# Chunk 0's output projection as seven block products woven into chunk 1, and the keys' copies of batch 2 on ScalarE

## The chip, the cores and the metric

The kernel runs on one core of one Trainium2 chip. The metric is the device time of one execution in microseconds (us). Executions of the same kernel mostly agree within 0.3%, so differences of half a microsecond need several rounds and, better, the trace. An execution that takes over 1.5% more than the fastest of the same kernel counts as slow and is left out of the comparisons; the others are called fast.

## The reference

The program is an attention whose keys and values are first averaged over groups of eight positions, followed by a gated feed-forward layer.

```python
batch, heads, seq, dim = 8, 8, 576, 64
k_p, v_p = mean over 8 positions of k, v            # 72 keys and values per head
attn = softmax(q @ k_p^T / sqrt(dim))               # with max subtraction
x = (attn @ v_p), heads side by side                # 4608 tokens x 512
out = (max(x @ w_gate, 0) * (x @ w_val)) @ w_out    # d_ff = 1536, float32 out
```

## The kernel before

The 4608 tokens are worked through in nine chunks of 512. Chunk c's gate and value products stand between the attention of batch c+1 (scores, values, transposes) and the output projection of chunk c-1.

A gate unit is eight products of 512 columns, a relu on ScalarE and a multiplication on VectorE. It takes two of four PSUM banks (`ps_mm`):

```python
def gate_val(c, fo, t0=0, n=TCH):
    ...
    for w in (wg_sb, wv_sb):
        t = ps_mm.tile([P, TCH], F32, name="mm_ps", tag="mm_ps")
        ... # matmuls of w with x_T into t
    nc.scalar.activation(out=relu[:, :n], in_=ps[0][:, :n], func=AF.Relu)
    nc.vector.tensor_tensor(out=h_tiles[c][:, fo, t0:t0 + n], in0=ps[1][:, :n], in1=relu[:, :n], op=ALU.mult)
```

From chunk 1 on the output projection is a 2x2 block product done with seven block products instead of eight (the scheme of Strassen and Winograd). It needs four differences of the weights (`weight_sums`, twelve VectorE operations, once) and four sums of blocks of h per chunk (eight VectorE operations with two operands in SBUF). One PSUM bank (`ps_acc`) holds the running product:

```python
def add(k, x, y, op, half):
    nc.vector.tensor_tensor(out=S[k][:, i], in0=x[:, i], in1=y[:, i], op=op)
...
def pr1():
    nc.scalar.copy(p1, product(a, e, True))
def pr2():
    nc.scalar.copy(rows[0][:, :, :HD], product(b, g, False))
def pr6():
    plus(u2, product(S[1], T[1], True), p1)
# pr7, pr4, pr5, pr3 follow in the same way, with VectorE additions
```

Chunk 0 alone used plain rows, twelve 512-column products per block of 128 tokens, in two halves (`o`), copied out by VectorE. At the handover from chunk 0 to chunk 1 the halves alternate with batch 1's last five pieces of values `V` and their transposes `x`:

```python
run([... pv[0], z[10], *Sc[14:], pv[1], z[11], V[4], o[0], V[0], x[4], o[1], V[1], x[0]])
q_dma(2)
run([o[2], V[2], x[1], o[3], x[2], V[3], o[4]])
prep_k(2, True)      # GpSimd: sums batch 2's keys, issues batch 3's loads
prep_v(2)            # GpSimd: sums batch 2's values
```

`z[i]` and `a[i]` are half gate units of chunk 0, `pv` the pooled values. A piece passes VectorE (reciprocal, multiplication), TensorE (transpose) and ScalarE (copy into `x_T`), and chunk 1's first gate unit needs x[4], x[0], x[1] and x[2].

The softmax here doesn't subtract the row's maximum and nothing guards it: scores larger than these inputs give would overflow.

Of the kernel before, what the change touches and what calls it, by code (L numbers as in the profile page):

```python
# [9 lines left out]
F32 = mybir.dt.float32  # L10
# [6 lines left out]
def kernel(  # L17
# [10 lines left out]
    nc = tc.nc  # L28
# [4 lines left out]
    DM = H * D  # L33
    DFF = moe_w_gate.shape[1]
    NTOK = B * S
    P = 128
# [200 lines left out]
    def run(pieces):  # L237
        for piece in pieces:
            piece()
# [26 lines left out]
    def k_transposes(b):  # L266
        ps = ps_mm.tile([P, KJ + 1, KROWS], F16, name="mm_ps", tag="mm_ps")
        k_windows(b, ps, 0, KJ + 1)
        eng = nc.scalar if b > 2 else nc.vector
        k_evacuate(b, ps, False, eng)  # L270
        k_evacuate(b, ps, True, eng)

# [183 lines left out]
        n, j = divmod(t, 2)  # L456
        eng.dma_start(out=out_cols_of[LAST, j, :, n * IQ:(n + 1) * IQ, cols], in_=o)

    def out_rows(c, ts, eng=None):

        cell = []

        def part(lo, hi):
            if not cell:
                cell.append(ps_mm.tile([P, DM], F32, name="mm_ps", tag="mm_ps"))
            t = cell[0]
            for fo in range(lo, hi):
                nc.tensor.matmul(  # L468
                    out=t, lhsT=h_tiles[c][:, fo, ts * P:(ts + 1) * P], rhs=wo_sb[:, fo, :],
                    start=(fo == 0), stop=(fo == n_fo - 1),  # L470
                )
            if hi == n_fo:
                o = fout_pool.tile([P, DM], F32, name="fout")
                if eng is nc.vector:
                    eng.tensor_copy(out=o, in_=t)
                else:
                    nc.scalar.copy(o, t)
                store(o, c * TCH + ts * P)

        return [lambda: part(0, n_fo // 2), lambda: part(n_fo // 2, n_fo)]  # L480



    sends = []
# [14 lines left out]
    def out_products(c, last=False):  # L499


        hc = h_tiles[c]
        a, d1 = hc[:, :n_hf, :HT], hc[:, :n_hf, HT:]
        b, d = hc[:, n_hf:, :HT], hc[:, n_hf:, HT:]
        S = [sum_pool.tile([P, n_hf, HT], F16, name=f"sum{i}") for i in range(4)]
        e, g, h = wo_sb[:, :n_hf, :HD], wo_sb[:, n_hf:, :HD], wo_sb[:, n_hf:, HD:]
        T = [wo_sums[:, i] for i in range(4)]
        p1, u2, u3 = [mid_pool.tile([P, 2, HD], F32, name=f"mid{i}") for i in range(3)]
        rows = [half_pool.tile([P, 2, DM], F32, name=f"rows{i}", bufs=2 - i) for i in range(2)]
        cell = {}  # L510

        def add(k, x, y, op, half):
            i = slice(half * n_hf // 2, (half + 1) * n_hf // 2)
            nc.vector.tensor_tensor(out=S[k][:, i], in0=x[:, i], in1=y[:, i], op=op)  # L514

        def product(lhs, rhs, first):
            if first:
                cell["ps"] = ps_acc.tile([P, 2, HD], F32, name="acc_ps", tag="acc_ps")
            ps = cell["ps"]
            for tb in range(2):  # L520
                for i in range(n_hf):

                    nc.tensor.matmul(  # L523
                        out=ps[:, tb, :], lhsT=lhs[:, i, tb * P:(tb + 1) * P], rhs=rhs[:, i, :],
                        start=(first and tb == 0 and i == 0), stop=(tb == 1 and i == n_hf - 1),
                        skip_group_check=True,
                    )
            return ps

        def plus(out_ap, x, y):  # L530
            nc.vector.tensor_tensor(out=out_ap, in0=x, in1=y, op=ALU.add)  # L531

        def send(half):

            def stores():
                for tb in range(2):
                    store(rows[half][:, tb, :], c * TCH + half * HT + tb * P)

            if c + 2 < n_chunks:
                sends.append(stores)  # L540
            else:
                stores()

        def pr1():
            nc.scalar.copy(p1, product(a, e, True))

        def pr2():
            nc.scalar.copy(rows[0][:, :, :HD], product(b, g, False))

        def pr6():  # L550
            plus(u2, product(S[1], T[1], True), p1)

        def pr7():
            plus(u3, product(S[2], T[2], False), p1)

        def pr4():
            if last:
                plus(rows[1][:, :, :HD], product(d, T[3], True), u3)
                send(1)
            else:  # L560
                plus(rows[1][:, :, :HD], product(d, T[3], False), p1)

        def pr5():
            plus(rows[1][:, :, HD:], product(S[0], T[0], True), u3)
            if not last:
                send(1)

        def pr3():
            plus(rows[0][:, :, HD:], product(S[3], h, False), u2)
            send(0)  # L570

        sums = [lambda k=k, x=x, y=y, op=op, half=half: add(k, x, y, op, half)
                for k, x, y, op in ((0, d1, d, ALU.add), (1, S[0], a, ALU.subtract),
                                    (2, a, d1, ALU.subtract), (3, b, S[1], ALU.subtract))
                for half in range(2)]
        order = [pr1, pr2, pr6, pr7, pr5, pr3, pr4] if last else \
            [pr1, pr2, pr6, pr7, pr4, pr5, pr3]
        return order, sums

    def last_products(c):  # L580
# [292 lines left out]
        trios = [Sc[i:i + 3] for i in range(0, 2 * H, 3)]  # L873
        return [[kt]] + [[]] * (b + 1 < B) + trios + [[p] for p in V], []

    def weave_units(units, others):

        n, m, seq = len(others), len(units), []
        for i, unit in enumerate(units):
            seq += [unit] + others[i * n // m:(i + 1) * n // m]  # L880
        return seq

    with tc.manual_schedule():
        nc.scalar.preload_act_table_set("natural_log_exp_and_others")
        nc.vector.memset(warm_sb, 0.0)
# [52 lines left out]
        half = TCH // 2  # L938
        a = [lambda fo=fo: gate_val(0, fo, 0, half) for fo in range(n_fo)]
        z = [lambda fo=fo: gate_val(0, fo, half, half) for fo in range(n_fo)]  # L940
        o = [p for ts in range(TCH // P) for p in out_rows(0, ts, nc.vector)]
        pv = [lambda half=half: pool_v_array(1, half) for half in range(2)]


# [36 lines left out]
        def kt():  # L981
# [7 lines left out]
        V = [lambda t=t: values(1, t) for t in range(n_pc)]  # L989
        x = [lambda t=t: back(1, t, nc.scalar) for t in range(n_pc)]  # L990

        run([z[3], z[4], z[5], a[6], qt[0], a[7], qt[1], qt[2], kt, z[6], z[7], a[8], *Sc[:4],
             z[8], *Sc[4:6], a[9], *Sc[6:8], z[9], *Sc[8:10], a[10], *Sc[10:12], a[11], *Sc[12:14],
             pv[0], z[10], *Sc[14:], pv[1], z[11], V[4], o[0], V[0], x[4], o[1], V[1], x[0]])
        q_dma(2)
        run([o[2], V[2], x[1], o[3], x[2], V[3], o[4]])
        prep_k(2, True)
        prep_v(2)

# [3 lines left out]
        for c in range(1, n_chunks):  # L1003
            gv = [lambda fo=fo: gate_val(c, fo) for fo in range(n_fo)]

            if c == 1:
                sums = weight_sums()
                units = weave_units(gv[:-1], o[5:])
            elif c < C_HIDDEN:
                prods, sums = out_products(c - 1)  # L1010
                units = []
                order = range(n_fo - 1)
                if c == C_HIDDEN - 1:

                    order = [fo for fo in range(n_fo) if fo % n_hf > 1]
                for fo in order:
                    if c == C_HIDDEN - 1 and len(prods) == 2:
                        units.append(gv[fo])
                        continue
                    units.append(gv[fo])  # L1020
                    if prods and fo not in (1, 4, 7, 10):
                        units.append(prods.pop(0))
            else:
                last = c == n_chunks - 1
                prods, sums = out_products(c - 1, last)
                units = []
                for fo in range(0, n_hf - 2 * last, 2):

                    if sums:
                        mine = [sums.pop(0) for _ in range(4)]  # L1030
                    else:
                        mine = x_sums_of(c + 1)
                    n = 2 if fo else 3
                    units += hidden_round(c, fo, prods[:n], mine)
                    del prods[:n]
                if last:

                    tail, last_sums = [], []

                    def begin_tail():  # L1040
                        products, ready = last_products(c)
                        tail.append(products)
                        last_sums.extend(ready)
                        run(ready[0])

                    units += [gv[n_hf - 2], prods.pop(0), begin_tail,
                              gv[n_fo - 2], lambda: run(last_sums[1]), prods.pop(0),
                              gv[n_hf - 1]]
                else:

                    gv[-1] = lambda: None
# [12 lines left out]
            for i, unit in enumerate(units):  # L1064
# [3 lines left out]
                    prep_v(c + 2)  # L1068
                unit()
                if c == 1:  # L1070
                    run(sums[i:i + 1])
                elif i in SUMS_AT and sums:
                    sums[SUMS_AT.index(i)]()
                if i in (0, 1) and sends:
# [45 lines left out]
```

## Time and profile before

| | before |
|---|---|
| median of 3 runs | 329.39 us (329.09 to 329.70) |
| profiled span | 327.4 us |
| first piece V[4] at TensorE | 49.32 us |
| chunk 1's first gate unit | 58.17 us |
| chunk 2's first gate unit | 87.34 us |

The three marks are starts of TensorE instructions in the timeline. They cut the span in four stages: what lies ahead, the handover (8.85 us), chunk 1 (29.17 us) and the rest (240.05 us).

One place shows why the keys' copies were to move. The timeline of VectorE before, then of TensorE (start, length, engine, line, operation, and in brackets the idle time with its releaser, that is, what ended it):

```profile
62.73 1.03 DVE L494 TENSOR_TENSOR wo_sums<-wo_sb 128x512 f16<-128x512 f16 x1
63.68 0.74 DVE L264 COPY kpT0l<-mm_ps 64x576 f16<-64x576 f16 x1
64.44 0.76 DVE L264 COPY kpT0u<-mm_ps 64x576 f16<-64x576 f16 x1
```

```profile
63.88 1.03 PE L430 MATMUL mm_ps<-x_T,wg_sb 128*128 128x512 f16 x4
65.26 1.04 PE L430 MATMUL mm_ps<-x_T,wv_sb 128*128 128x512 f16 x4 [0.35 <-DVE kpT0u L264]
```

The copies stand behind a weight sum. The bank that they empty is the one that the value half of the fourth gate unit needs, so TensorE stands still for 0.35 us. A bracket understates a delay, because rows of TensorE overlap in this view. A row of four 512-column products is listed with 1.03 us, but without a wait the next row starts 0.86 us after its start.

### The profile page before, as it was taken

The page shows a single profiled execution, that of the slowest core. Times are in us where ns is not written, and L with a number is a line of the kernel's source. Part 1 is how long each engine was busy: PE and PEld are TensorE (multiplying, and loading weights), DVE is VectorE, ACT ScalarE, POOL GpSimd, SP SyncE. Part 2 cuts the span into 40 slices and gives each one's busy share as a digit, 9 for nine tenths or more (in the row PEclk, how much of TensorE's full clock was granted, in tenths as well). Part 3 has the DMA queues.
Part 4 walks back from the last instruction along what each step waited for, and adds up shares of the span by engine and source line. Part 5 has one row for each costly group of instructions (what it writes and reads, how often), then busy time and mean ns, then how long its engine had stood idle before and what let it go on. Part 6 is the DMA issues. An engine that isn't in the chain of part 4 may idle for free.

```text
span 327.4 us, 7013 instructions
## 1 busy us (share of the span) xinstructions
PE 318.7 (97%) x2670; PEld 226.9 (69%) x2670; DVE 226.2 (69%) x482; ACT 151.2 (46%) x353; POOL 206.9 (63%) x258
## 2 busy tenths in 40 slices
PE   8899999999999999999999999999999999999995
PEld 3577885455566656665898867655667888888674
DVE  7465737677684864696387745784779989879762
ACT  1454482364466226612672257225825565565330
POOL 8556607999999942965199309999901577667300
PEclk9999999999999999999999999999999999999999
DMA  7999998996958538999794472223012130130035
GB/s 110 186 203 202 200 211 151 200 173 118 187 101 159 100 91 86 78 154 160 159 169 76 87 104 60 33 47 124 3 24 50 34 96 2 22 111 2 10 112 137
DMA packets 51010, 35.46 MB, mean 108 GB/s; under 512 B 30432, under 2 KB 45024, under 8 KB 50976
## 3 DMA queue, kind: packets, MB, share of 16 engines
q0 software_dynamic: 18304, 18.88, 36.5%
q1 hardware_dynamic: 32528, 16.00, 26.2%
q8 instruction: 21, 0.34, 0.4%
q10 hardware_dynamic: 144, 0.13, 0.1%
q14 instruction: 13, 0.11, 0.1%
HBM read 37.75 MB, written 9.44 MB: 144 GB/s over the span
## 4 chain that ended last, share of the span: by engine, by line
PE 89%; DVE 6%; DMA 2%; issue 1%; POOL 1%; ACT 0%; DVEq 0%; POOLq 0%
PE mm_ps L430 42%; PE acc_ps L523 19%; PE mm_ps L742 9%; PE at_ps L311 4%; PE mm_ps L468 3%; PE at_ps L389 3%; PE mm_ps L602 2%; DMA q<-in_q_dram 2%; PE at_ps L742 2%; DVE px L395 1%; DVE sum L514 1%; DVE h L439 1%; PE mm_ps L412 1%; PE mm_ps L366 1%; DVE px L758 1%
## 5 line engine op out<-in xcount | busy, mean ns | idle before, releaser
L439 DVE TENSOR_TENSOR h<-mm_ps,relu 128x512 f16<-128x512 f32 (+1 forms) x96 | 59.8, 624 | 69.5 <-PE mm_ps L430 59.2
L436 ACT ACTIVATE relu<-mm_ps 128x512 f16<-128x512 f32 (+1 forms) x96 | 52.2, 544 | 100.1 <-PE mm_ps L430 94.6
L430 PE MATMUL mm_ps<-x_T,wv_sb 128*128 128x512 f16 (+1 forms) x432 | 88.4, 332 | 0.4 <-DVE kpT0u L264 0.4
L430 PE MATMUL mm_ps<-x_T,wg_sb 128*128 128x512 f16 (+1 forms) x432 | 88.5, 331 | 0.0
L430 PEld LDWEIGHTS <-wv_sb 128*128 128x128 f16 x432 | 42.1, 98 | 31.2 <-DVE kpT0u L264 0.8
L430 PEld LDWEIGHTS <-wg_sb 128*128 128x128 f16 x432 | 38.9, 97 | 19.7 <-issue 0.3
L325 ACT ACTIVATE expT<-at_ps 72x288 f16<-72x288 f32 (+2 forms) x128 | 38.8, 374 | 14.3 <-PE at_ps L311 14.2
L523 PEld LDWEIGHTS <-sum 128*128 128x128 f16 x336 | 32.0, 98 | 6.3 <-DVE sum L514 0.9
L395 DVE TENSOR_TENSOR px<-at_ps,prd 128x256 f16<-128x256 f32 (+1 forms) x80 | 33.8, 423 | 2.7
L181 POOL TENSOR_TENSOR tree_b<-tree_a 72x256 f32<-72x256 f32 (+1 forms) x42 | 33.5, 797 | 3.3
L764 POOL TENSOR_TENSOR h<-px 128x256 f16<-128x256 f16 x36 | 25.4, 718 | 13.8 <-ACT px L761 12.8
L175 POOL TENSOR_TENSOR tree_a<-k_in 96x512 f32<-96x512 f16 x18 | 21.5, 1196 | 15.2 <-DMA k_in<-in_k_dram 15.2
L523 PE MATMUL acc_ps<-wo_sums,sum 128*128 128x256 f16 x252 | 30.9, 272 | 0.0
L175 POOL TENSOR_TENSOR tree_a<-v_in 72x512 f32<-72x512 f16 x24 | 28.7, 1197 | 0.1
L523 PEld LDWEIGHTS <-h 128*128 128x128 f16 x252 | 23.7, 98 | 2.9
L763 POOL TENSOR_SCALAR px<-px 128x256 f16<-128x256 f16 x12 | 13.0, 1080 | 18.1 <-PE mm_ps L742 15.3
L844 POOL COPY gate<-h 128x1 f16<-128x1 f16 x4 | 1.5, 380 | 33.9 <-DVE h L439 33.9
L523 PE MATMUL acc_ps<-wo_sb,h 128*128 128x256 f16 x168 | 20.6, 272 | 0.0
L514 DVE TENSOR_TENSOR sum<-h 128x768 f16<-128x768 f16 x28 | 19.0, 679 | 0.0
L531 DVE TENSOR_TENSOR rows<-acc_ps,mid 128x512 f32<-128x512 f32 x21 | 14.4, 686 | 4.7 <-PE acc_ps L523 4.6
L389 PEld LDWEIGHTS <-expT 72*128 72x128 f16 (+1 forms) x280 | 12.9, 100 | 5.9 <-DVE prd L394 0.8
L394 DVE RECIPROCAL prd<-at_ps 128x4 f32<-128x4 f32 (+1 forms) x80 | 13.7, 171 | 3.7 <-PE at_ps L389 3.6
(144 smaller groups left out, 527.9 us busy)
## 6 DMA issues: line engine op xcount, KB each, us to landing
out_dram<-rows SPq DMA_DIRECT2D x24, 256.0 KB
k_in<-in_k_dram POOLq DMA_DIRECT2D x7, 576.0 KB, 7.0
q<-in_q_dram POOLq DMA_DIRECT2D x7, 576.0 KB, 10.0
v_in<-in_v_dram POOLq DMA_DIRECT2D x6, 576.0 KB, 12.7
wg_sb<-in_moe_w_gate_dram POOLq DMA_DIRECT2D x6, 256.0 KB, 11.0
wv_sb<-in_moe_w_val_dram POOLq DMA_DIRECT2D x6, 256.0 KB, 10.8
wo_sb<-in_moe_w_out_dram POOLq DMA_DIRECT2D x3, 512.0 KB, 10.7
v_in<-in_v_dram POOLq DMA_DIRECT2D x2, 512.0 KB, 11.9
```

The source lines that it names most:

```text
L175: eng.tensor_tensor(out=cell["a"][:n], in0=src[:, :, :4 * D], in1=src[:, :, 4 * D:], op=ALU.add)
L181: eng.tensor_tensor(out=cell["c"][:n], in0=a[:n, :, :2 * D], in1=a[:n, :, 2 * D:], op=ALU.add)
L325: nc.scalar.activation(out=out_ap, in_=in_ap, func=AF.Exp, scale=EXP_SCALE)
L389: nc.tensor.matmul(out=ps[:n, c0:c0 + D + 1], lhsT=weights(b, h, t), rhs=stats[b % 2][:SP, g, s0:s0 + D + 1], start=True, stop=True,)
L395: nc.vector.tensor_tensor(out=x[:n, half * NG // 2:(half + 1) * NG // 2, :, :], in0=pv.rearrange("p g (x c) -> p g x c", x=2)[:, :, :, :D] ...
L430: nc.tensor.matmul(out=t[:, lo:hi], lhsT=w[:, ci, fsl], rhs=x_T[:, ci, x0:x0 + hi - lo], start=(ci == 0), stop=(ci == n_co - 1),)
L436: nc.scalar.activation(out=relu[:, :n], in_=ps[0][:, :n], func=AF.Relu)
L439: nc.vector.tensor_tensor(out=h_tiles[c][:, fo, t0:t0 + n], in0=ps[1][:, :n], in1=relu[:, :n], op=ALU.mult)
L514: nc.vector.tensor_tensor(out=S[k][:, i], in0=x[:, i], in1=y[:, i], op=op)
L523: nc.tensor.matmul(out=ps[:, tb, :], lhsT=lhs[:, i, tb * P:(tb + 1) * P], rhs=rhs[:, i, :], start=(first and tb == 0 and i == 0), stop=(tb ...
L742: nc.tensor.matmul(out=ps[key][:, m], lhsT=w_of(m)[:, i], rhs=xs[:, i], start=(first and m == 0 and i == 0), stop=(m == 1 and i == N_CO - ...
L764: nc.gpsimd.tensor_tensor(out=hc[:, fo_out, cols], in0=gv[:, 0], in1=gv[:, 1], op=ALU.mult)
```

## The change

The intent is to save an eighth of chunk 0's projection work on TensorE and to free VectorE of the keys' copies. The first two products are cut into four parts of six matmuls, which take the old halves' place in the handover; the other five go whole between chunk 1's gate units. Half of the weight sums moves ahead, into chunk 0. The sums of h go behind chunk 1's first units.

```diff
 def k_transposes(b):
-        eng = nc.scalar if b > 2 else nc.vector
+        eng = nc.scalar
 ...
+        if c == 0:
+            order[:2] = [lambda pr=pr, tb=tb: pr((tb,)) for pr in order[:2] for tb in range(2)]
 ...
-             pv[0], z[10], *Sc[14:], pv[1], z[11], V[4], o[0], V[0], x[4], o[1], V[1], x[0]])
+             pv[0], *w_sum[:3], z[10], *Sc[14:], pv[1], *w_sum[3:6], z[11], V[4]])
+        prods, sums = out_products(0)
+        run([prods[0], V[0], x[4], prods[1], V[1], x[0]])
         q_dma(2)
-        run([o[2], V[2], x[1], o[3], x[2], V[3], o[4]])
+        run([prods[2], V[2], x[1], prods[3], x[2], V[3]])
 ...
-                units = weave_units(gv[:-1], o[5:])
+                units = gv[:4] + prods[4:5] + gv[4:6] + prods[5:6] + gv[6:8] + prods[6:7] + \
+                    gv[8:9] + prods[7:8] + gv[9:11] + prods[8:]
+                at = [sums[:2], sums[2:3], sums[3:4], w_sum[6:7], [w_sum[7], sums[4]],
+                      [w_sum[8], sums[5]], w_sum[9:10], w_sum[10:11], w_sum[11:], [], [], [],
+                      sums[6:7], sums[7:]]
 ...  # out_rows and weave_units removed; pr1 and pr2 take a list of blocks
-                    run(sums[i:i + 1])
+                    run(at[i] if i < len(at) else [])
```

`at[i]` is what VectorE gets behind unit i: `sums[:2]`, two sums of h, come behind chunk 1's very first gate unit.

More of the change, by code (lines that the diff above doesn't have):

```diff
@@ L457, in store_cols @@
         eng.dma_start(out=out_cols_of[LAST, j, :, n * IQ:(n + 1) * IQ, cols], in_=o)
-    def out_rows(c, ts, eng=None):
-        cell = []
-        def part(lo, hi):
-            if not cell:
-                cell.append(ps_mm.tile([P, DM], F32, name="mm_ps", tag="mm_ps"))
-            t = cell[0]
-            for fo in range(lo, hi):
-                nc.tensor.matmul(
-                    out=t, lhsT=h_tiles[c][:, fo, ts * P:(ts + 1) * P], rhs=wo_sb[:, fo, :],
-                    start=(fo == 0), stop=(fo == n_fo - 1),
-                )
-            if hi == n_fo:
-                o = fout_pool.tile([P, DM], F32, name="fout")
-                if eng is nc.vector:
-                    eng.tensor_copy(out=o, in_=t)
-                else:
-                    nc.scalar.copy(o, t)
-                store(o, c * TCH + ts * P)
-        return [lambda: part(0, n_fo // 2), lambda: part(n_fo // 2, n_fo)]
     sends = []
@@ L514, in add, with product @@
             nc.vector.tensor_tensor(out=S[k][:, i], in0=x[:, i], in1=y[:, i], op=op)
-        def product(lhs, rhs, first):
-            if first:
+        def product(lhs, rhs, first, blocks=(0, 1)):
+            if first and 0 in blocks:
                 cell["ps"] = ps_acc.tile([P, 2, HD], F32, name="acc_ps", tag="acc_ps")
             ps = cell["ps"]
-            for tb in range(2):
+            for tb in blocks:
                 for i in range(n_hf):
@@ L542, in send, with pr1, pr2 @@
                 stores()
-        def pr1():
-            nc.scalar.copy(p1, product(a, e, True))
-        def pr2():
-            nc.scalar.copy(rows[0][:, :, :HD], product(b, g, False))
+        def pr1(blocks=(0, 1)):
+            ps = product(a, e, True, blocks)
+            if 1 in blocks:
+                nc.scalar.copy(p1, ps)
+        def pr2(blocks=(0, 1)):
+            ps = product(b, g, False, blocks)
+            if 1 in blocks:
+                nc.scalar.copy(rows[0][:, :, :HD], ps)
         def pr6():
@@ L874, in attention @@
         return [[kt]] + [[]] * (b + 1 < B) + trios + [[p] for p in V], []
-    def weave_units(units, others):
-        n, m, seq = len(others), len(units), []
-        for i, unit in enumerate(units):
-            seq += [unit] + others[i * n // m:(i + 1) * n // m]
-        return seq
     with tc.manual_schedule():
@@ L940 @@
         z = [lambda fo=fo: gate_val(0, fo, half, half) for fo in range(n_fo)]
-        o = [p for ts in range(TCH // P) for p in out_rows(0, ts, nc.vector)]
         pv = [lambda half=half: pool_v_array(1, half) for half in range(2)]
@@ L990 @@
         x = [lambda t=t: back(1, t, nc.scalar) for t in range(n_pc)]
+        w_sum = weight_sums()
         run([z[3], z[4], z[5], a[6], qt[0], a[7], qt[1], qt[2], kt, z[6], z[7], a[8], *Sc[:4],
              z[8], *Sc[4:6], a[9], *Sc[6:8], z[9], *Sc[8:10], a[10], *Sc[10:12], a[11], *Sc[12:14],
-             pv[0], z[10], *Sc[14:], pv[1], z[11], V[4], o[0], V[0], x[4], o[1], V[1], x[0]])
+             pv[0], *w_sum[:3], z[10], *Sc[14:], pv[1], *w_sum[3:6], z[11], V[4]])
+        prods, sums = out_products(0)
+        run([prods[0], V[0], x[4], prods[1], V[1], x[0]])
         q_dma(2)
-        run([o[2], V[2], x[1], o[3], x[2], V[3], o[4]])
+        run([prods[2], V[2], x[1], prods[3], x[2], V[3]])
         prep_k(2, True)
@@ L1006 @@
             if c == 1:
-                sums = weight_sums()
-                units = weave_units(gv[:-1], o[5:])
+                units = gv[:4] + prods[4:5] + gv[4:6] + prods[5:6] + gv[6:8] + prods[6:7] + \
[3 more added lines that the diff above has]
+                      sums[6:7], sums[7:]]
             elif c < C_HIDDEN:
```

## The prediction

> **What bounds the kernel now.** I read the page first. Its busy line and its clock row say that TensorE sets the time and that no throttle disturbs it:
>
> ```profile
> PE 318.7 (97%) x2670; PEld 226.9 (69%) x2670; DVE 226.2 (69%) x482; ACT 151.2 (46%) x353; POOL 206.9 (63%) x258
> ...
> PE   8899999999999999999999999999999999999995
> ...
> PEclk9999999999999999999999999999999999999999
> ```
>
> The reader is to see that in all of the 40 slices but the first and the last TensorE is at least nine tenths busy. So a change pays only if it takes TensorE work away, or one of the few TensorE gaps, and does not open new ones. Next I asked for the waits between 40 and 120 us, where chunk 0's output projection lies:
>
> ```profile
> PE mm_ps L430 <- DVE kpT0u L264: 0.4, 1, 0.4
> ...
> PE at_ps L311 <- ACT expT L325: 0.2, 1, 0.2
> ```
>
> These are the only two TensorE waits there: one gap of 0.35 us at 65.26 us (a gate product waits for a PSUM bank that the copy of batch 2's keys holds), and 0.2 us that the change does not touch. Then I read the chain of work in order of time, where each piece is one run of TensorE instructions (start, length, line, count):
>
> ```profile
> 53.51 1.29 PE mm_ps L468 x6
> 54.80 0.25 PE at_ps L389 x8
> 55.05 0.23 PE mm_ps L412 x4
> 55.27 1.29 PE mm_ps L468 x6
> 56.57 0.22 PE mm_ps L412 x4
> 56.79 0.25 PE at_ps L389 x8
> 57.04 1.30 PE mm_ps L468 x6
> 58.34 1.73 PE mm_ps L430 x8
> ```
>
> L468 is half of a row block of the old output projection: six 512-column products in 1.30 us, 216 ns each. L389 computes one piece of attention values, L412 transposes a piece, L430 is the first gate and value unit of chunk 1. Before 58 us the old halves serve as filler: each 1.30 us covers the time in which VectorE normalises a piece and ScalarE copies its transpose.
>
> **What the Trainium skill says.** "TensorE: Matmul & The Clock Gate", section "Back-to-back issue gap", gives N/2.4 + 2.5 ns for a warm matmul of N columns: 216 ns for 512 and 109 for 256. The trace agrees with both: 1.30/6 = 216 ns here, and the seven-product form of later chunks takes 1.31 us for its twelve 256-column products, 109 ns each. The saving is therefore the plain arithmetic one. The same page's table at the top says that VectorE and ScalarE work strictly in order; this trace fits it (at 62.73 us a weight sum stands ahead of the keys' copies, which start at 63.68), and it is why I place every added operation in a queue. "SBUF — State Buffer", section "Who interferes with whom", says that a VectorE instruction with two SBUF inputs contends with GpSimd's reads. The trace fits: the weight sums take 0.416 us at best and 1.106 at worst while GpSimd works.
>
> **The change part by part.**
>
> *TensorE work.* Removed: 8 halves x 1.30 = 10.40 us. Added: 7 products x 1.31 = 9.17 us. Net -1.23 us.
>
> *The keys' copies of batch 2.* They leave VectorE, where they ran from 63.68 to 65.20 (0.74 + 0.76 us) behind a 1.03 us weight sum. On ScalarE such a copy takes 0.63 us (the row of batch 3 at 89.57), and at that moment ScalarE only has a 0.60 us relu every 1.73 us. Two copies end some 1.3 us after the transposes, so the 0.35 us gap should go: -0.35 us.
>
> *VectorE.* In the stretch 58 to 87 us it is busy 20.7 us of 29. Leaving: two copies of keys (1.5), three of four row copies in some part (about 1.4 of them in this stretch, at 0.69), and half of the weight sums (six at a mean of 0.67 = 4.0), which move to 46 to 49 us. Coming: eight sums of h at 0.68 (5.4) and five additions from PSUM at 0.69 (3.4). 20.7 - 6.9 + 8.8 = 22.6 us, 72% of a stretch of some 31.5 us; chunk 2, which already runs this form, has 23.0 of 32 and no gap above 0.3 us. So VectorE should keep up.
>
> *The early weight sums.* At 46.1 and 48.0 us VectorE has idle times of 1.48 and 1.49 us; GpSimd is idle there too, so three sums at 0.42 = 1.26 us fit in each. The second three need the last third of the output weights. Its landing is given as 8.9 to 12.5 us after issues at 33.6 to 35.1, that is 47.6 at the latest: just in time, without margin.
>
> *The handover from chunk 0 to chunk 1, 49.3 to 58.2 us.* Here the choice lies. Before, five halves (6.5 us) stand between five pieces of values and four transposes. After, only four half products of six 256-column matmuls, 0.655 us each, 2.6 us. TensorE's own work is then 4.9 us, but the pieces now wait for each other. I followed the queues with the trace's durations: reciprocal and multiply of one piece take VectorE 1.11 us at the least; a piece is ready 1.52 us after its first product (0.33 until VectorE starts, 1.19 until the second multiply ends); a transposed piece is in place 1.0 us after its transposes start (0.42 + 0.58); a ScalarE copy out of PSUM takes 0.60 and starts 0.2 after its products.
> - First piece 49.32, half product 49.70 to 50.36, second piece to 50.63, its transpose waits for VectorE until 51.05: +0.4.
> - The fourth six products, which add onto the same bank, wait for ScalarE's copy of the first product (52.13 to 52.73): the third half product starts at 52.78, +0.37.
> - The transposes of the piece that chunk 1 needs last start at 55.0, +0.45; ScalarE copies the second product (54.77 to 55.37) ahead of them, so they are in place at 56.0, and the first gate unit waits from 55.47: +0.58.
>
> It starts at 56.05 instead of 58.17: 2.12 us gained, of 3.9 that were taken out; 1.8 us return as gaps. Later the five whole products of 1.31 us replace three halves of 1.30: +2.65 us.
>
> *Sum.* -2.12 + 2.65 - 0.35 = +0.18 us. If no gap appeared it would be -1.58.
>
> *Stores.* Chunk 0's stores move to the start of chunk 2. Stores are not waited for by TensorE, and the transpose of batch 2's queries may then be issued before its 54.69 us. I count 0.
>
> **The rivals.**
> 1. *The saving arrives whole*: -1.23 - 0.35, 327.8 us. For it: TensorE bounds the kernel everywhere else. Against it: VectorE alone needs 5 x 1.11 us for the pieces, so the gate unit can hardly start before 55.45 and at least 1.2 us of gaps must appear. Even with ideal queues, -0.4 us, 329.0.
> 2. *The gaps take the place of the work removed* (my choice): 329.6, or a little less if my latencies are each a tenth too long.
> 3. *VectorE becomes the bound in chunk 1*: two sums of h lie in the first slots (0.69 + 2 x 0.68 = 2.05 us against a unit of 1.73), and with contention a sum took up to 1.3 us. A gate unit waits when the unit two before it is not yet multiplied. This could add 0.3 to 1 us: 330 to 330.6. Against it: chunk 2's even profile, and product units that need no gate bank stand between.
> 4. *The early weight sums wait for their transfer*: VectorE then stands still ahead of the last multiply of chunk 0 and of the first piece, and everything after shifts, up to 1 us. For it: no margin. Against it: the write traffic before 48 us is unchanged.
>
> **Range and chances.** The terms known well (-1.23, -0.35) nearly cancel against gaps of 1.2 to 2.3 us. I shade rival 2 slightly towards fewer gaps and add rivals 3 and 4 with small weight: 329.3 us, range 328.3 to 330.3. The whole effect is bounded by the 10.4 us that are exchanged and by some 2 us of gaps either way, while 2% are 6.6 us; so within 2% with 0.98, and 0.01 for each side.
>
> **What would show it.** In the changed kernel's chain of waits: new TensorE waits between 49 and 57 us, on the pieces (L395's successor), on ScalarE's first product copy, and on the last transposed piece, 1.2 to 2.3 us together; the first 512-column gate unit at 55.5 to 56.5; no wait for the keys' copy; the twelve-product pieces at 1.31 us; VectorE at about 72% from there to chunk 2's start, which should come within 0.6 us of the present 87.3. I am wrong if the first gate unit starts before 55.4 or after 57, if TensorE waits for VectorE's sums in chunk 1 by more than 0.5 us, or if a later stage gains or loses by itself.

## The result and the profile after

The changed kernel takes 330.1 us (median of 6 runs, 329.69 to 330.51) against 329.05 of the kernel before (6 runs, 328.94 to 329.70). The ratio is 1.0027, with a 95% interval of 1.0014 to 1.0040. Ratios here are the mean time of one kernel's fast runs over that of the other's fast runs of the same rounds, so not quite the ratio of the medians. The change costs about 0.9 us: the same within 2%, slower by a quarter of a percent, and inside the predicted range, though the predicted middle, 329.3, was 0.1 us under the time that the prediction started from, not 0.9 over it.

Busy lines of the page after, to be held against the one in the prediction:

```profile
PE 318.2 (97%) x2706; PEld 230.5 (70%) x2706; DVE 231.7 (71%) x489; ACT 153.7 (47%) x357; POOL 208.5 (63%) x258
```

TensorE is busy 0.5 us less, VectorE 5.5 us more. The 0.5 does not contradict the predicted 1.23: at each wait the 0.17 us by which rows otherwise overlap counts as busy time of its own, and between 49 and 90 us there are five waits in place of one, so -1.23 + 4 x 0.17 = -0.55 us is to be expected (an estimate from the rows' lengths and distances). Where the time went is told by the stages:

| stage, us | before | after | difference |
|---|---|---|---|
| up to V[4] | 49.32 | 49.53 | +0.21 |
| handover | 8.85 | 6.58 | -2.27 |
| chunk 1 | 29.17 | 32.25 | +3.08 |
| the rest | 240.05 | 240.08 | +0.03 |

The first line is not put down to the change. TensorE's program is the same up to there, though VectorE's already holds six more weight sums. In the eight profiles whose first stage holds the same TensorE work this mark lies between 49.24 and 49.68. And in the changed kernel TensorE's wait for the first queries ends at 9.13 us instead of 8.93, which is 0.20 of the 0.21 ahead of any changed instruction. TensorE's waits between 40 and 120 us, after (total in us, how often, the longest):

```profile
PE mm_ps L430 <- DVE h L439: 0.8, 1, 0.8
PE mm_ps L430 <- ACT x_T L414: 0.4, 1, 0.4
PE at_ps L311 <- ACT expT L325: 0.2, 1, 0.2
PE acc_ps L500 <- ACT mid L524: 0.2, 1, 0.2
PE mm_ps L412 <- DVE px L395: 0.2, 1, 0.2
```

The wait for the keys' copies is gone. Three of the new ones lie in the handover, as the timeline of TensorE there shows (L389 is a piece's values, L412 its transposes, L500 six products of the new projection):

```profile
51.43 0.83 PE L500 MATMUL acc_ps<-wo_sb,h 128*128 128x256 f16 x6
52.09 0.41 PE L389 MATMUL at_ps<-stat,expT 72*128 72x65 f16 x8
52.34 0.39 PE L412 MATMUL mm_ps<-ident,px 128*128 128x128 f16 x4
52.93 0.81 PE L500 MATMUL acc_ps<-wo_sb,h 128*128 128x256 f16 x6 [0.20 <-ACT mid L524]
53.58 0.41 PE L389 MATMUL at_ps<-stat,expT 72*128 72x65 f16 x8
53.83 0.39 PE L412 MATMUL mm_ps<-ident,px 128*128 128x128 f16 x4
54.05 0.82 PE L500 MATMUL acc_ps<-wo_sb,h 128*128 128x256 f16 x6
54.71 0.28 PE L412 MATMUL mm_ps<-ident,px 128*128 128x128 f16 x2
55.15 0.28 PE L412 MATMUL mm_ps<-ident,px 128*128 128x128 f16 x2 [0.17 <-DVE px L395]
55.27 0.41 PE L389 MATMUL at_ps<-stat,expT 72*128 72x65 f16 x8
56.11 1.02 PE L430 MATMUL mm_ps<-x_T,wg_sb 128*128 128x512 f16 x4 [0.42 <-ACT x_T L414]
```

The reader is to see a chain with too little beside it: the transposes of the last piece are cut in two at 54.71 and 55.15 because VectorE has half of that piece ready at 55.1 only, and the gate unit then waits for ScalarE's copy of it. Counted from start to start as above, this last wait delays TensorE by 0.59 us: the gate unit was due 0.25 us after 55.27 and starts at 56.11.

The largest wait, 0.8 us, lies in chunk 1. VectorE's timeline there, and GpSimd's of the same time:

```profile
58.11 0.69 DVE L439 TENSOR_TENSOR h<-mm_ps,relu 128x512 f16<-128x512 f32 x1 [1.31 <-PE mm_ps L430]
58.72 3.40 DVE L491 TENSOR_TENSOR sum<-h 128x768 f16<-128x768 f16 x2
62.03 0.68 DVE L439 TENSOR_TENSOR h<-mm_ps,relu 128x512 f16<-128x512 f32 x1
```

```profile
58.63 0.87 POOL L132 DMA_DIRECT2D v_in<-in_v_dram  x1
59.52 1.17 POOL L175 TENSOR_TENSOR tree_a<-v_in 72x512 f32<-72x512 f16 x1
60.77 0.93 POOL L181 TENSOR_TENSOR tree_b<-tree_a 72x256 f32<-72x256 f32 x1
```

The two sums of h take 3.40 us, 2.40 the first and 1.07 the second; alone such a sum takes 0.55. The first ends at 61.11, 0.42 us after GpSimd's tree_a (59.52 + 1.17 = 60.69). The multiplication of the second gate unit, ready at about 60, therefore starts at 62.03, and the fourth gate unit, which needs its bank, at 62.77 after 0.79 us of waiting; from start to start (60.95 to 62.77, less 0.86) that is a delay of 0.96 us.

### The profile page after: what moved, and what is told of

It is laid out like the page before. It is cut to its first block, busy times and chain, and to the rows that moved or that the text cites. A ratio compares the mean times of both kernels' runs of the same rounds, so it can differ in the third digit from the quotient of the medians.

```text
span 328.4 us, 7099 instructions
## 1 busy us (share of the span) xinstructions
PE 318.2 (97%) x2706; PEld 230.5 (70%) x2706; DVE 231.7 (71%) x489; ACT 153.7 (47%) x357; POOL 208.5 (63%) x258
## 4 chain that ended last, share of the span: by engine, by line
PE 86%; DVE 7%; DMA 2%; issue 2%; ACT 2%; POOL 1%; DVEq 0%; ACTq 0%; POOLq 0%
PE mm_ps L430 41%; PE acc_ps L500 21%; PE mm_ps L726 8%; PE at_ps L311 4%; PE at_ps L389 3%; PE mm_ps L586 2%; DVE sum L491 2%; DVE px L395 2%; DMA q<-in_q_dram 2%; PE at_ps L726 2%; DVE h L439 1%; DVE px L742 1%; PE mm_ps L282 1%; PE mm_ps L412 1%; PE mm_ps L342 1%
## 5 line engine op out<-in xcount | busy, mean ns | idle before, releaser
L500 PEld LDWEIGHTS <-sum 128*128 128x128 f16 x384 | 36.6, 98 | 7.1 <-DVE sum L491 0.9
L500 PE MATMUL acc_ps<-wo_sums,sum 128*128 128x256 f16 x288 | 35.4, 272 | 0.0
L500 PEld LDWEIGHTS <-h 128*128 128x128 f16 x288 | 27.0, 98 | 3.6 <-issue 0.3
L491 DVE TENSOR_TENSOR sum<-h 128x768 f16<-128x768 f16 x32 | 24.3, 761 | 0.0
L500 PE MATMUL acc_ps<-wo_sb,h 128*128 128x256 f16 x192 | 23.9, 272 | 0.2 <-ACT mid L524 0.2
L508 DVE TENSOR_TENSOR rows<-acc_ps,mid 128x512 f32<-128x512 f32 x24 | 16.5, 687 | 5.3 <-PE acc_ps L500 5.1
L389 PEld LDWEIGHTS <-expT 72*128 72x128 f16 (+1 forms) x280 | 12.9, 100 | 5.0 <-DVE prd L394 0.8
```

Source lines behind the costliest of these rows:

```text
L389: nc.tensor.matmul(out=ps[:n, c0:c0 + D + 1], lhsT=weights(b, h, t), rhs=stats[b % 2][:SP, g, s0:s0 + D + 1], start=True, stop=True,)
L500: nc.tensor.matmul(out=ps[:, tb, :], lhsT=lhs[:, i, tb * P:(tb + 1) * P], rhs=rhs[:, i, :], start=(first and tb == 0 and i == 0), stop=(tb ...
```

## The experiments

Each was timed in five rounds against the kernel before. Kernels share a chip: the first four below, the next four, and the two pairs at the end. Except in after_again, the changed kernel was not in the same rounds: it is compared by its ratio to the kernel before, 1.0027. Stages are from the profile of each run.

**Theory.** The change loses in two places what it saves on TensorE: gaps in the handover, for want of independent TensorE work, and VectorE's sums of h, which GpSimd holds up. **Rivals.** The keys' copies on ScalarE delay relus; the sums are slow of themselves or for a transfer; ScalarE's copies of the first two products are what makes the handover late.

### keys_only: the kernel before with that one part

```diff
-        eng = nc.scalar if b > 2 else nc.vector
+        eng = nc.scalar
```

> The kernel before with one part of the change alone: batch 2's keys copied on ScalarE. Theory (that part is worth the gap it removes): the 0.35 us gap at 65 us goes, no other opens, time 0.3 to 0.4 us under the kernel before. Rival (two more ScalarE copies delay the relus of the gate units and open a new gap): same time as before or slower.

Chunk 1 shrank from 29.17 to 28.64 us, and of TensorE's waits between 40 and 120 us only the old 0.2 us is left:

```profile
PE at_ps L311 <- ACT expT L325: 0.2, 1, 0.2
```

The ratio is 1.0003 (0.998 to 1.0025): too wide to see half a microsecond; one run of 336.05 fell out of the fast ones. So by the trace this part is worth 0.53 us, which is the about 0.52 us of delay from start to start (63.88 to 65.26 in the kernel before, less 0.86) behind the 0.35 us gap, and the rival has nothing for it. By time alone the run is inconclusive.

### keys_back: the changed kernel without that part

```diff
-        eng = nc.scalar
+        eng = nc.scalar if b > 2 else nc.vector
```

> The changed kernel with the keys' copies of batch 2 put back on VectorE. Theory (VectorE is the late engine at 58 to 65 us because of the sums of h): the copies queue behind the sums, end near 65.4 us, and the fourth gate unit waits for their bank: 1 to 2 us slower than the changed kernel, some 331.5 us. Rival (the keys' place does not matter to the new form): within 0.4 us of the changed kernel.

The ratio to the kernel before is 1.0057 (1.0030 to 1.0084), the median 330.33 us. Chunk 1 took 34.08 us, 1.83 more than after. VectorE's copies came as expected behind the sums:

```profile
62.44 1.31 DVE L491 TENSOR_TENSOR sum<-sum,h 128x768 f16<-128x768 f16 x1
63.67 0.74 DVE L264 COPY kpT0l<-mm_ps 64x576 f16<-64x576 f16 x1
64.45 0.76 DVE L264 COPY kpT0u<-mm_ps 64x576 f16<-64x576 f16 x1
```

But they held up something else than expected. The fourth gate unit waits 0.77 us for VectorE's multiplication, as in the changed kernel; it is the scores of batch 2 that then wait 0.48 us for the keys, and two products wait 0.41 and 0.23 us for sums of h. The profile fell on a long execution (332.59 us); four of the six took 329.69 to 330.33 and two over 332. By the ratios the loss is 0.3%, about 1 us, at the lower end of what was expected, but the intervals overlap, and the median lies 0.98 us over the kernel before, where the changed kernel's lay 1.05 over it. So one trace shows the keys' place costing 1.83 us of chunk 1, and the times do not settle whether this is so in most executions.

### pool_held: GpSimd waits for the first two sums

```diff
-        prep_k(2, True)
-        prep_v(2)
+        prep_k(2, False)
 ...  # behind unit 0 of chunk 1, after its sums:
+        nc.gpsimd.tensor_copy(out=gate, in_=sum_tiles[0][0][:, n_hf - 1, :1])
+        load_k(3); load_q(3); load_v(3)
+        prep_v(2)
```

> The changed kernel with GpSimd made to wait for the first two sums of h (a one-column copy that reads the sum) before it issues batch 3's loads and sums batch 2's values. Theory (the first sum took 2.40 us because GpSimd held what both share): both sums take 0.55 to 0.6 us, the 0.79 us wait of the third gate unit's successor goes, time 0.7 to 0.8 us under the changed kernel unless later loads come too late. Rival (the sum is slow of itself, or for a transfer): the sum keeps over 1.5 us and the time does not move.

Nothing of VectorE's program changed. Its timeline:

```profile
58.25 0.69 DVE L439 TENSOR_TENSOR h<-mm_ps,relu 128x512 f16<-128x512 f32 x1 [1.32 <-PE mm_ps L430]
58.86 1.02 DVE L492 TENSOR_TENSOR sum<-h 128x768 f16<-128x768 f16 x2
60.20 0.69 DVE L439 TENSOR_TENSOR h<-mm_ps,relu 128x512 f16<-128x512 f32 x1 [0.32 <-PE mm_ps L430]
```

The two sums took 1.02 us instead of 3.40, the 0.8 us wait is gone, and chunk 1 took 31.34 us instead of 32.25. The time is that of the kernel before: ratio 1.0001 (0.9987 to 1.0014), 0.26% less than the changed kernel's ratio. The loads of batch 3, issued some 2.5 us later, were not missed. So GpSimd's work was the cause of the 2.40 us, and that cost is worth 0.9 us. This edit holds back loads and additions together, so by itself it does not tell GpSimd's additions from the transfers. The traces of all 14 profiles do: of the sums of h ahead of 215 us, 62 took over 1.25 us, and the 59 of these that overlapped a tree_a addition all ended 0.41 to 0.43 us after it. The other three overlapped loads being issued (see the last section).

### sum_early: one of the two sums moved ahead

```diff
-             ... a[10], *Sc[10:12], a[11], *Sc[12:14],
+             ... a[10], sums[0], *Sc[10:12], a[11], *Sc[12:14],
-                at = [sums[:2], ...
+                at = [sums[1:2], ...
```

> The changed kernel with one of the two first sums moved ahead of the handover, into an idle time of VectorE near 45 us where GpSimd is idle. Theory (two contended sums in one slot are what the 0.79 us gap comes from): that sum takes 0.55 us there, the gap shrinks to 0 to 0.2 us, time 0.6 to 0.8 us under the changed kernel. Rival (the gap is due to something else in chunk 1's first units, such as the keys' copies delaying relus): the gap stays over 0.5 us.

The moved sum takes 0.55 us at 45.09, where GpSimd is idle. The other still takes 1.92 us, but the wait is gone and chunk 1 took 31.30 us, the same as with GpSimd held. In the time almost nothing shows: ratio 1.0022 (1.0008 to 1.0036). The rest of the kernel took 240.68 us, 0.60 more than after, with the same instructions. TensorE's waits after 90 us, sum_early:

```profile
PE acc_ps L500 <- DVE sum L491: 0.6, 2, 0.3
```

In the changed kernel this line reads 0.3 us, once, near 221 us; the second wait here is at 152.33 us, 0.30 us for a sum that took 1.31. Matching TensorE's instructions one by one, the lead of 0.97 us falls to 0.82 at 96 us and to 0.37 at 152 us. So the mechanism is confirmed for chunk 1, and the gain was lost again: later sums met GpSimd at another moment. The expectation for the time was a miss.

### copy_late: ScalarE's copy of the second product moved back

```diff
-        run([prods[2], V[2], x[1], prods[3], x[2], V[3]])
+        run([prods[2], V[2], x[1], prods[3], x[2], lambda: prods.pop()(), V[3]])   # the copy is split off
```

> The changed kernel with ScalarE's copy of the second product moved behind the copy of the last transposed piece. The working of the prediction (that copy stands ahead of the piece and costs most of the 0.58 us it gave to the last gap): the 0.42 us wait of the first gate unit goes, time 0.4 us under the changed kernel. Rival, read from the trace after (the transposes themselves end only when the copy ends, because VectorE finishes the piece at 55.1): the wait stays within 0.1 us of 0.42.

The handover took 6.57 us and the wait for x_T stayed at 0.4 us; ratio 1.0030 (1.0015 to 1.0044). ScalarE now copies the piece at 55.24, after an idle time:

```profile
54.02 0.59 ACT L414 COPY x_T<-mm_ps 128x512 f16<-128x512 f16 x1 [0.89 <-PE mm_ps L412]
55.24 0.59 ACT L414 COPY x_T<-mm_ps 128x512 f16<-128x512 f16 x1 [0.63 <-PE mm_ps L412]
55.72 0.59 ACT L529 COPY rows<-acc_ps 128x512 f32<-128x512 f32 x1
```

The product copy cost nothing: the piece itself arrives late. The prediction's words, that ScalarE copies the second product "ahead of them, so they are in place at 56.0", named the wrong cause. Its sum did not need that copy: transposes from 55.0 and 1.0 us to be in place give 56.0 alone.

### filler: a gate unit of chunk 0 moved into the handover

```diff
-             pv[0], *w_sum[:3], z[10], *Sc[14:], pv[1], *w_sum[3:6], z[11], V[4]])
+             pv[0], *w_sum[:3], pv[1], *w_sum[3:6], z[10], *Sc[14:], V[4]])
-        run([prods[0], V[0], x[4], prods[1], V[1], x[0]])
+        run([prods[0], V[0], x[4], prods[1], V[1], x[0], V[2]])
-        run([prods[2], V[2], x[1], prods[3], x[2], V[3]])
+        run([z[11], x[1], prods[2], x[2], prods[3], V[3]])
```

> The changed kernel with chunk 0's last gate unit moved into the handover and the pieces' order adapted, no work added or removed. Theory (the handover is bound by the chain VectorE to TensorE to ScalarE of five pieces; TensorE idles there for want of independent work): from the first piece to chunk 1's first gate unit there is less idle, that gate unit starts 0.7 to 1.1 us earlier, time lower by as much unless the contended sums take it back. Rival (VectorE's own throughput of 1.1 us a piece is the only limit and more TensorE work there does not help): gate unit no earlier than 55.8 us.

The handover now holds 0.87 us more TensorE work (52.47 to 53.34) and takes 6.82 us, so its idle time fell by some 0.6 us. Chunk 1's first gate unit starts at 55.35 us, without a wait, straight after the last piece's values:

```profile
55.10 0.41 PE L389 MATMUL at_ps<-stat,expT 72*128 72x65 f16 x8
55.35 1.03 PE L430 MATMUL mm_ps<-x_T,wg_sb 128*128 128x512 f16 x4
```

Over all profiles of both orders that unit starts at a mean of 56.02 us without the filler (six) and 55.19 with it (six). The theory holds: with independent work in it the handover idles less. The edit also moves pieces and transposes, and no run separates that from the added work. Ratio 1.0009 (0.9995 to 1.0023); the rest took 240.67. Chunk 1 is no shorter than after (32.21 us), but the loss sits elsewhere: here the first two sums took 0.55 us each, and a product waits in its middle for a later sum of 1.07 us that stands behind a weight sum of 1.19:

```profile
70.35 1.16 PE L500 MATMUL acc_ps<-wo_sums,sum 128*128 128x256 f16 x9 [0.73 <-DVE sum L491]
```

So it is not one pair of sums alone that can cost chunk 1 its 0.9 us. Which one does depends on how VectorE and GpSimd meet.

### early_filler and held_filler

The first combines the filler with five of the eight sums moved to idle times of VectorE ahead of the handover (39.4 to 43.5 us in its trace); the second combines it with the held GpSimd.

> The changed kernel with the last gate unit as filler and five of the eight sums of h moved to idle times of VectorE between 40 and 46 us, where GpSimd does nothing. Theory (handover gaps and contended sums are all that the change lost): the moved sums take 0.55 us each, both gaps go, time 1.5 to 2 us under the changed kernel, that is 0.6 to 1.1 us under the kernel before. Rival (gaps come back in a later stage, as 0.7 us did with one sum moved): less than 1 us under the changed kernel.

> The changed kernel with the last gate unit as filler and GpSimd held behind the first sums. Theory: the two gains add, 1.5 to 2 us under the changed kernel. Rival (with the handover shorter the held loads or values come too late in chunk 1 or 2): under 1 us.

In early_filler each moved sum took 0.55 us. Stages of handover, chunk 1 and rest: 6.82, 31.31, 240.77 and 6.82, 31.33, 240.29 us. Ratios: 0.9993 (0.9978 to 1.0008) and 0.9983 (0.9968 to 0.9997). Chunk 1's gap and the first gate unit's wait are gone in both. early_filler gives 0.7 us back in the rest, as its rival said; by the ratios it is 0.34% under the changed kernel, about 1.1 us, short of the theory's 1.5 and just over the rival's 1. held_filler is 0.44% under the changed kernel by the ratios, about 1.4 us, a little under the expected 1.5.

### after_again and all_three

after_again is the changed kernel unedited; all_three joins filler, early sums and held GpSimd.

> The changed kernel once more, unchanged, so that it and the best version stand in the same rounds. Theory: 0.2 to 0.4% over the kernel before, and the first sum of h again well over 1.5 us in the profile with a wait of 0.6 to 1 us behind it. Rival (that sum's 2.40 us was chance): the wait is missing and the time is that of the kernel before.

> The changed kernel with the filler, five early sums, and GpSimd held behind the one sum that is left in the first slot. Theory (in chunk 1 and in the handover nothing more is to be had once the gaps are gone): 1.2 to 1.8 us under the changed kernel, no more than 0.3 us from the version with filler and held GpSimd. Rival (contended sums still cost in chunk 1 there): a further 0.5 us under that version.

This pair ran among unsteady executions: even the kernel before had one of 337.01 and one of 330.34 us. after_again had a median of 330.09 and a ratio of 1.0050 (1.0014 to 1.0085). In its profile it was the second sum that took 2.35 us, the first 0.55, and the wait behind them was 0.2 us; chunk 1 took 31.95 us. So a sum of 2.4 us is no chance (keys_back and copy_late have one of 2.38 and 2.49), but which sum it is, and whether 0.2 or 0.8 us of it reaches TensorE, changes between executions; my expectation of at least 0.6 was a miss.

all_three gave 329.20 to 336.99 us, median 332.44; by its fast runs the ratio is 1.0073 (1.0020 to 1.0126), slower than the kernel before and a clear miss of what was expected. Its profile shows a TensorE wait of 1.4 us for a DMA transpose in chunk 4 that no other profile has:

```profile
PE mm_ps L430 <- DMA x_T<-px: 1.4, 1, 1.4
```

In chunk 2, products also waited twice, 0.41 and 0.47 us. Its chunk 1 took 31.31 us, no less than with two of the edits. It was not run again, so whether the three edits together or the unsteady rounds made it slow is open; the two runs below repeat only its parts.

### held_filler2 and early_filler2

> The version with filler and held GpSimd a second time, because the run of the version with all three edits fell among unsteady runs and showed a late DMA transpose in chunk 4. Theory (its gain is real): 0.1 to 0.4% under the kernel before again, no DMA wait in the profile. Rival (holding GpSimd makes a later transfer late in some executions): times spread over 2 us, a TensorE wait on a DMA in the profile.

> The version with filler and five early sums (GpSimd not held) a second time, in the same rounds. Theory: within 0.2% of the kernel before or under it, spread no wider than that kernel's. Rival (early sums are what made the version with all three edits unsteady): times spread over 2 us.

held_filler2: median 328.10 us (327.84 to 329.15), ratio 0.9992 (0.9977 to 1.0007). early_filler2: 328.80 us (328.32 to 329.59), ratio 1.0007 (0.9995 to 1.0019). Neither is unsteady, and neither profile has a wait for a DMA in chunk 4. Filler with held GpSimd was the lower of the two in both sets of rounds, though the intervals overlap: 0.1 to 0.2% under the kernel before, of which one set excludes a tie and the other does not, and some 0.4% under the changed kernel.

| stage, us | handover | chunk 1 | rest |
|---|---|---|---|
| before | 8.85 | 29.17 | 240.05 |
| keys_only | 8.85 | 28.64 | 240.04 |
| after | 6.58 | 32.25 | 240.08 |
| after_again | 6.57 | 31.95 | 240.41 |
| pool_held | 6.57 | 31.34 | 239.84 |
| sum_early | 6.57 | 31.30 | 240.68 |
| filler | 6.82 | 32.21 | 240.67 |
| held_filler | 6.82 | 31.33 | 240.29 |
| held_filler2 | 6.82 | 31.34 | 239.84 |

## Why the prediction was right or wrong

- **The readings.** Some are wrong, and only the first bears on the result. That "with contention a sum took up to 1.3 us" holds for the trace up to 120 us alone. Later the kernel before has a sum of 1.95 us, the second of the two in the first line here, at the same load issue and addition as the changed kernel's long sum. TensorE is under nine tenths in the second of the 40 slices too. Two of the four row copies, not three, lie in the stretch from 58 to 87 us (68.01 and 85.59), which gives the 1.4 us that the sum uses. And "the fourth six products" in the working are the third half product.

```profile
130.38 2.41 DVE L514 TENSOR_TENSOR sum<-sum,h 128x768 f16<-128x768 f16 x2
130.33 0.85 POOL L132 DMA_DIRECT2D v_in<-in_v_dram  x1
131.21 1.17 POOL L175 TENSOR_TENSOR tree_a<-v_in 72x512 f32<-72x512 f16 x1
```

- **TensorE's saving.** Right: twelve products took 1.31 us wherever they stand in chunk 1. The formula that the prediction quotes from "TensorE: Matmul & The Clock Gate" stands in its section "Back-to-back issue gap" as the gap of an isolated product; for a sustained stream the section gives about 131 ns at 512 columns. The stream here took 216 ns each, so the measurement sides with the formula. Chunk 1 without contended sums, 31.30 to 31.34 us, is keys_only's 28.64 plus the predicted 2.65, that is 31.29.
- **The keys' copies.** Right in kind: the gap went and no TensorE wait for a relu came up. 0.53 us of chunk 1 instead of 0.35, by keys_only: the prediction took the idle time for the delay.
- **The handover.** Right in size and order: -2.27 us against -2.12. From start to start the four delays measure 0.26, 0.37, 0.34 and 0.59 us where the working has 0.40, 0.37, 0.45 and 0.58, in all 1.56 us of the 1.80. Wrong in one cause that it names for the last, ScalarE's second product copy: copy_late took that copy away and the gap stayed. filler showed what closes it.
- **The early weight sums.** They fitted in VectorE's idle times, 1.09 us for each three, and waited for no transfer. Rival 4 did not happen.
- **VectorE in chunk 1: the term that was mis-sized.** The prediction counted eight sums "at 0.68 (5.4)" and 22.6 us of VectorE work, and concluded that "VectorE should keep up". After, VectorE is busy 26.0 us of chunk 1's 32.25, and the first two sums alone took 3.40 us where I had 1.36. Where it asked whether VectorE keeps up, I had averaged over sums that meet GpSimd and sums that don't; this pair starts just when GpSimd issues batch 3's loads and begins on the values. That is rival 3: expected to add 0.3 to 1 us with a small weight, it adds 0.95 over the 31.30 us without it. The chunk's own figure, 72% of VectorE's time, came out as 81%, and said nothing of two operations in one slot of 1.73 us.
- **By its own signs.** The first gate unit (56.11 us) and the rest (+0.03) came as said. But the prediction called itself wrong if TensorE waits for VectorE's sums in chunk 1 by more than 0.5 us, and it waited 0.79; chunk 2 starts at 88.36, 1.0 us later than before, not within 0.6. The main choice, rival 2, gave 329.6. That the measured 330.1 still lies in the range, 0.2 us from its end, is due to the room left for rival 3, and not to the chosen account alone.
- **The sum.** -2.27 + 2.65 - 0.53 + 0.95 = +0.80 us from the change. With +0.21 from the start and +0.03 from the rest this is the 1.0 us between the profiled spans, and near the 0.9 us of the timed runs.

Open: the kernel before itself falls into two groups about 0.8 us apart in later rounds (for instance 328.44 to 328.65 and 329.01 to 329.45 us), and the stage after chunk 1 takes 239.84 to 240.79 us in all profiles but all_three's, with the same instructions. In sum_early, the lead is lost near 96 us (a wait of 0.09 us for a piece) and at 152 us (0.30 us for a sum), which from start to start cost 0.15 and 0.47 us and so account for its extra 0.6 us. Whether such waits explain the two groups of the kernel before no run shows.

## What to carry to other kernels

When work is taken out between the links of a chain that passes several engines, the work was also filler: count what independent work is left beside each link before counting the saving. An operation of VectorE with two SBUF operands had no fixed cost here where GpSimd works (0.55 to 2.49 us for the same sum); price it with what GpSimd does at that moment, and rather move it to a time when GpSimd is idle, or hold GpSimd for a microsecond, than put two into one slot. A gain shown in one stage can be lost in a later one by a mere shift of two engines against each other, so read all stages before believing a local repair. And price a delay from start to start, not by the idle time that the profile shows.

## What the Trainium skill lacked or had wrong

- "SBUF — State Buffer", section "Who interferes with whom", gives contention of two-input VectorE instructions with GpSimd's reads, but no size. Here a sum of 0.55 us took up to 1.50 us in the changed kernel where it met one or two GpSimd additions, and over all profiles 1.66 to 2.49 us where a DMA issue or a further addition came ahead. Ahead of 215 us, 59 of the 62 over 1.25 us ended 0.41 to 0.43 us after the addition that they had to sit out.
- The same section infers that a `tensor_tensor` does not meet GpSimd's descriptor generation. Three sums speak against it: in pool_held one started at 101.56 us and took 1.39 us while GpSimd only issued loads (101.56 to 102.97), and one in held_filler and one in held_filler2 took 1.38 and 1.40 us in the same place. Another sum, at 60.81 us in pool_held, overlapped such issues and took 0.55, so it is not every issue that holds a sum, and no run isolates what does.
- The same section says that issue order decides who blocks. The changed kernel's long sum started at 58.72 us, ahead of the addition at 59.52, and ended after it; in the kernel before, the sum of 1.95 us did the same (start 130.85, the addition at 131.21). Which part of GpSimd's work held it at first is not settled here.
- No page has the filler's point in numbers: removing 3.9 us of TensorE work from the handover shortened it by 2.27 us, and moving 0.87 us of independent work there started the next chunk 0.83 us earlier.
